# Attention with a sliding window and a mixing layer on one core: DMA transposes of q and k in three parts per batch, and batch 1's transposes in two bank pairs

## The chip, the cores and the metric

The kernel runs on one core of one Trainium2 chip. A time is the device time of one execution in microseconds; the kernel before took 301.77 us (median of 4 executions, 301.3 to 301.95). Engines are named as in the profile: PE is the matrix engine, PEld its weight load, DVE, ACT and POOL the vector, scalar and GpSimd engines, SP the engine that here only issues DMAs. Lines (L768) are those of the kernel before.

## The reference

Inputs are q, k and v of 8 batches, 8 heads, 576 positions and 64 head dimensions in float32, and two weights. Attention looks at most 127 positions back, with a bias that falls linearly with the distance; its output is the input of a two-layer block with g = h cos h between the layers.

```python
scores = scale * np.matmul(q, k.transpose(0, 1, 3, 2))
mask = (rel >= 0) & (rel < window)                    # window = 128
scores = np.where(mask, scores + bias[None], -1000000000.0)
attn = softmax(scores)
x = np.matmul(attn, v).transpose(0, 2, 1, 3).reshape(B * S, H * D)   # 4608 x 512
h = x @ w_in                                          # 512 -> 2048
out = (h * np.cos(h)) @ w_out                         # 2048 -> 512
```

## The kernel before

**Attention.** The 576 positions of a batch are four blocks of 128 and one of 64. The work is cut into units: a unit (b, pr, G) is batch b, a pair of heads pr, and two query blocks, 0 and 1 for G = 0, 2 and 3 for G = 1; a ninth unit (b, "t", None) is the tail, block 4 for all heads. A block of queries sees only its own block of keys and the one before. So G = 0 reads key blocks 0 and 1, G = 1 reads 1, 2 and 3, the tail reads 3 and 4. For each unit PE makes the scores (L538, the tail at L528), ACT takes the exponential (L568, L560), DVE multiplies by a mask with the bias in it (L592, L579), PE multiplies by v (L623 and L626, the tail L610 and L612), DVE divides by the sum (L664, L679, L652). The result xnat or xtail is brought to xT, channels on partitions, either by PE transposes (L692, L730) with an eviction (L702, L703, L739, L740), or by a DMA transpose from SP (`x_dma`, L753, the tail L748).

**The two layers.** They go over 9 chunks of 512 tokens. Chunk 0's first layer is `moe1_half` (L792) in halves of 256 tokens, the others `moe1` (L768); ACT makes the cosine (L774, L797), DVE the product gT (L778, L801). Chunk 0's second layer is plain (L853); the others use a scheme with seven products in place of eight (L909) and sums of gT and w_out made on DVE. SP stores the results (L865, L954).

**q and k.** The scores need them with the head dimension on partitions, in the tiles qt and kt (two of each, by the batch's parity). Batches 0 and 1 are loaded as rows and transposed on PE by `qk_transposes` (L481: blocks of 16 or 20 transposes into two PSUM banks, evicted at L498 or L499). From batch 2 on, POOL loads q and k with a conversion to bf16 (`load_nat`, L339, five DMAs each into qnat and knat), and SP issues two DMA transposes for each (`dma_transposes`): L350 for the four full blocks of all four head pairs, 16 blocks of 128 x 128, and L353 for the 64 positions of the tail. Both count on one semaphore, and the key `("tr", which, b % 2)` stands for both: `tkeys` makes every scores operation of the batch wait for the whole q and the whole k. `load_nat` of batch b + 2 writes over qnat and knat of batch b, so it waits for b's transposes; for batch 3 it waits for batch 2's transposes by an explicit key (L343).

**Order.** Each call of `op` records an operation with the keys that it reads and writes. Nothing is scheduled at run time: the table `STARTS` holds a start for each operation and, where an operation may run on ACT or DVE, which of the two. `Plan.schedule` sorts by it, and `Plan.emit` writes each engine's instructions in that order, with semaphore waits where the keys ask for them. Every engine works strictly in its order, SP and POOL (which issue the DMAs) too.

Of the kernel before, what the change touches and what calls it, by code (L numbers as in the profile page):

```python
# [16 lines left out]
NBLK = 5  # L17
# [13 lines left out]
    "c-pO24RBP|72cOXa(x5(I4W)~i!PU!n68h_l0Nn)ci$#JvTT>Qh5<sb{46Q06ag_HP0@nHLTijMGE9d;#FQ$-pI~Q%qT-BFY"  # L31
    "cW#GD1!*tv9_RN!730;7P7DBy<IjxyHU&ZC42Y0bI-l^obP<++_eaL+;Z(nNjm=Fn{E-hvv26ov#utlbwS5Rz**D4Fw`x*pT"
    "UBV^`+(7ocZasXYy75rdI*~@V_gyWw)jG2H!=pWYA@ZG2>cuRv5@Gp1~`N9uu;Y?k8>az8(mA2LG}y8DnmDmXKv07aJt#!dG"
    "b#T<xzIe5LQZkY(xYtI59Ro!-mSxEWTr8CvgIy<c2?HTnQ!iXs`~y*B9S7z<ffg|CyW=^i*+18UL~@&1aev~36X#RmzN9m|L"
    "h%0hq4uNR*Te9$uty#ng)CCAJ(4T>9B33!wc6NG+o_j|YGbpG$)WnW3t#QL$Tub(~45lmS~VkM;6q-!h#Xs|qVQ?F;LQ&eUp"
    "8dP`6COh6EW2X=jSr<AJSf!WD_3$c9A@paOklWGUCbu)g`n3Kfq;x`WXN7NEo9XHPj%$TXf$2T?3WgK8U-wWc7Ef8`=obc?T"
    "XdRv64G7j?$5+QSH3*~mT#-$tengJO$K#lWTGX>#O}1+GHZkZ>)346i3_dgP8=LJ&>7s7GRwBaQgT*zSE53MEB_DDr9FdU{j"
    "0GLyUkFNcXK9KdhEYTfeHf`XtJC40y$X@F>{5Wr`25iI#`jW$oV?0mv^OM)HOgq?(UWG-nmX$3IpGSee{AEwh;T)tLM6|t2E"
    "?<^rF9<=4>xF(cZWmu4#JYc(1aEe`APoOIExO=~M2<Q+^BAzSI1Rr?tim8eAXGfJHn5U{yu>`?oQfna`Ic1qF8NvYf3s(e1J"
    "DA4)zHOAc-M4Scrk@ldEN6xvebYB{>~Y^`Iq{>5y)cD(<lGW}FpS((2C2b>RuR@c2}eXYiJXwmKaXTl+vl7A+!oY|a=%_)*P"  # L40
    "1HKXG3(v8R+{ny#JW{7TY(&?nyMvD{TR8pHc=?!gxBV@-U7ku8d-gn%-%`Ma16?JZ*8Z&y2Qo{At=e8jL_*xu%105=FM=di@"
    "jnA99e}zUP+)|JRz6G;32H>^<Z&tiLW$^{JkqulP!<FHY1~6R>D^w!|49rxLW=oZAhLw>RNIUyQV5l|^S?>72F(5Tp&ca+RO"
    "TIM9f%Oc$|r_Oq5<DLw`+?>zZ#95XkRjvZL{s1_2gKXI(n4TJCXWtE|Mx_n;IHhIKu-KOmc^PQJU?OD)K9Q;Ot&+;HAAEsw{"
    "~b(%X+8w?`W&tC0X|K$U{kAOS0m19b#g<044~30(y59NS4iaiLd|gED*bkz0bHdWIUPUhZyV;AUs-f#PCRFuo5YHK4sv6LdH"
    "6iPdjP0quU7v>xX_T-dgW@hiCHiqh4%XQ1?Hrouv=hbPFsH7cI_(+8m%!ka%deDKXhpUNwK8$?;V6P;k=S8w%tF9wg(w}O+$"
    "z$Dq_^iHPsQ7Go;6^DyH|CI-o!ynzh!?oTJN00M>oNqItta{zsFyr;t+m1#*cYTQ98VNNA5Q+8OdlQnBROj(ZT9q=A@ne075"
    "M>%QM6sDr5DWGjNez{Vvdu`PXd8Q`&?z!e^5PN-wKg~1HS&NVV(LX{1#t(8>4cJlDlo?9)>F#(%W4ZW@hLIZxJ|oA)cR)Lv3"
    "<F^llvG{Gd_C(Kvb&$rr3E=HH8V<?->O<UkuU$#=l|_aB6=92KI@Q)N-(wu14tXeCo-=OUBt6>7rNeGe8;Ra*w5#<`%&uCKr"
    "eAypX`h9h&EAK~c-U&j$`Y5N-d6N)3D*e6{M_C!r&uRR?d3ZjME7nH7CExOhl&3M=F(SOd##QaFi?4ZrhFeM}Uw2T>+lcM=i"
    "#3)8@$FAy88Q$$!$Kumn`Q!wVC3yM4FG7yKAt{_wq-`bZb;3At!%8Z@ZDn<Q*8C-fG2+Ypcf-E)h$=;uom1q}LC~NV(QFaI#"  # L50
    "crKL`<eP+T#J3kY<K`ogQFi`VvFu>l2gsR|+H7;5*AOelH$&uvQ=5oPL#zr9@Ba(kZ#(i-5j^?*9ctAw*JB>=&7b2A4c$q*e"
    "9|4>FFa8F!Io(I-ukV-zGsZ}rXkI>?Z4Qvo$f7y=jUJe9C>Bm{%BO+u+hGvWTR6Hd=}jx88L$ihjqS;h}EZ{kw*BQgB0;>go"
    "+Z~h$Dp()Ho@T5#Ji8h;))5XtPm+VtErQ@yo{U#f`(Hd;)1)Jn67ZT$K2oHny~YP<4^}%R)lToeTI56?+ji_;qXIDAL5Apy*"
    "Q-9a6x#SRIN`_n}bfJ=lvxhv>BPJi<&vyY{I_B|}vBTw*Sj?OZn{1_eCV=wn7bXp7BqA)=k%WS$}6X<dd2=NX@8_{|JE0cRE"
# [166 lines left out]
def bass_alibi_sliding__then__act_gcu_kernel(  # L221
# [8 lines left out]
    with ExitStack() as ctx:  # L230
# [104 lines left out]
        def load_nat(which, src, b):  # L335
            fns = []
            for t in range(NBLK):
# [6 lines left out]
               dma=f"ldn{which}{b % 2}", occ=4400, lat=4500)  # L344

        def dma_transposes(b):
            for which in ("q", "k"):
                t = tr[which][b % 2][:, :].rearrange("p (c k t) -> p c k t", c=NBLK, k=NPAIR)
                fns = [
                    lambda e, t=t, which=which: e.dma_start_transpose(  # L350
# [769 lines left out]
```

The softmax here doesn't subtract the row's maximum and nothing guards it: scores larger than these inputs give would overflow.

## Time and profile before

| | |
|---|---|
| median of 4 executions | 301.77 us (301.3 to 301.95) |
| the profiled execution | 301.95 us, of which the span from first to last instruction is 300.2 |
| TensorE clock granted | 1.000 |
| busy: PE, DVE, ACT, POOL | 292.9, 240.5, 209.5, 95.0 us |
| software queue (POOL's DMAs) | 99344 packets, 18.10 MB |
| hardware queue (SP's DMAs) | 48976 packets, 19.54 MB |
| DMA transposes of q and k | 24: 12 of 16 blocks, 12 of the tail |
| qt, from issue to landing (min, median, max) | 2.4, 7.8, 13.2 us |
| kt, the same | 2.4, 7.4, 13.7 us |

How to read it: busy time and what ended the idle time stand by line and engine. The chain of work that ended last is followed back from the last instruction, at each step to what released it; "issue" in it is time in which the profile shows no engine that was waited for. A DMA is issued by SP or POOL, and the time in which the queue is busy with the issue (SPq) is not the time of the transfer: that ends with the landing. By stretches of the execution (columns: length, busy us and instructions of each engine, granted clock, mean busy DMA share, GB/s):

```profile
0.00:24.00 24.00, 20.39 (x270) 13.52 (x271) 16.02 (x52) 18.90 (x31) 22.42 (x36) 1.00 1.26 177
24.00:72.00 48.00, 48.00 (x468) 29.34 (x467) 38.00 (x71) 35.49 (x52) 18.82 (x23) 1.00 1.74 177
72.00:125.00 53.00, 52.89 (x599) 37.33 (x593) 46.66 (x99) 40.18 (x54) 29.59 (x37) 1.00 1.88 161
125.00:185.00 60.00, 59.38 (x664) 45.94 (x663) 53.17 (x107) 46.48 (x63) 24.16 (x29) 1.00 1.61 139
185.00:260.00 75.00, 74.87 (x659) 47.80 (x658) 60.36 (x110) 50.61 (x71) 0.00 (x0) 1.00 0.37 74
260.00:300.00 40.00, 37.35 (x279) 26.90 (x277) 26.24 (x44) 17.82 (x32) 0.00 (x0) 1.00 0.22 73
```

The first column of each bracketed pair is PE, then PEld, DVE, ACT and POOL.

### The profile page before, as it was taken

What the parts mean: (1) busy time and instruction counts of PE and PEld (TensorE: products, weight loads), DVE (VectorE), ACT (ScalarE), POOL (GpSimd) and SP (SyncE); (2) the same over time, 40 slices, a digit from 0 to 9 for tenths busy, and PEclk for the clock granted to TensorE, in tenths of its full rate; (3) what the DMA queues carried; (4) which work ended last, traced back from release to release, by engine and by line L of the source; (5) the groups of instructions that cost most, each with busy time, mean ns of one, the idle gap of its engine ahead of it and who ended that gap; (6) DMA issues with size and microseconds to landing.
All of it is one profiled execution on the core that took longest, in us unless ns stands there. A gap on an engine that the chain in (4) does not pass through costs nothing.

```text
span 300.2 us, 7125 instructions
## 1 busy us (share of the span) xinstructions
PE 292.9 (98%) x2925; PEld 200.8 (67%) x2925; DVE 240.5 (80%) x478; ACT 209.5 (70%) x300; POOL 95.0 (32%) x122
## 2 busy tenths in 40 slices
PE   8889999999999999999999999999999999999996
PEld 4568746547774688548888876568746865566685
DVE  3787678789977998899988879788978967685871
ACT  6887977398857788588768775778676945644432
POOL 7998230069956502760196004000000000000000
PEclk9999999999999999999999999999999999999999
DMA  7999999999999999999999999942304111120033
GB/s 142 181 200 210 206 165 174 145 160 186 172 133 138 174 156 178 159 173 167 139 110 144 147 115 158 159 78 64 98 27 99 44 30 52 37 76 31 0 124 122
DMA packets 148352, 38.09 MB, mean 127 GB/s; under 512 B 133984, under 2 KB 147040, under 8 KB 148320
## 3 DMA queue, kind: packets, MB, share of 16 engines
q0 software_dynamic: 99344, 18.10, 78.7%
q1 hardware_dynamic: 48976, 19.54, 36.0%
q8 instruction: 23, 0.38, 0.5%
q14 instruction: 9, 0.07, 0.1%
HBM read 36.70 MB, written 9.44 MB: 154 GB/s over the span
## 4 chain that ended last, share of the span: by engine, by line
PE 94%; DVE 2%; DMA 1%; issue 1%; ACT 0%; DVEq 0%; ACTq 0%
PE ps L768 37%; PE ps L909 33%; PE ps L538 5%; PE ps L792 5%; PE ps L853 5%; PE ps L623 3%; PE ps L626 2%; PE ps L481 2%; DMA ob<-in_q_dram 1%; PE ps L692 1%; PE ps L528 1%; PE ps L610 1%; PE ps L612 1%; DVE xnat L664 1%; DVE xT L740 0%
## 5 line engine op out<-in xcount | busy, mean ns | idle before, releaser
L768 PE MATMUL ps<-xT,w_inb 128*128 128x512 bf16 (+1 forms) x576 | 129.8, 356 | 0.0
L774 ACT ACTIVATE cos<-ps,halfpi 128x512 f32<-128x512 f32 x128 | 82.3, 686 | 46.3 <-PE ps L768 34.9
L778 DVE TENSOR_TENSOR gT<-ps,cos 128x512 f16<-128x512 f32 x128 | 83.0, 685 | 21.6 <-ACT cos L774 21.1
L768 PEld LDWEIGHTS ps<-xT,w_inb 128*128 128x128 bf16 x576 | 55.1, 98 | 39.8 <-DVE xnat L679 0.8
L568 ACT ACTIVATE p<-ps 128x768 bf16<-128x768 f32 (+1 forms) x64 | 55.6, 917 | 8.5 <-PE ps L538 7.5
L329 POOL DMA_DIRECT2D vp<-in_v_dram x40 | 34.0, 872 | 64.1 <-PE ps L626 51.2
L909 PE MATMUL ps<-wsum,gT 128*128 128x256 f16 x256 | 50.8, 273 | 0.1
L592 DVE TENSOR_TENSOR p<-p,emask 128x512 bf16<-128x512 bf16 (+2 forms) x88 | 39.0, 470 | 3.7 <-ACT p L568 3.3
L909 PE MATMUL ps<-w_outb,gT 128*128 128x256 f16 x256 | 39.7, 273 | 0.0
L909 PE MATMUL ps<-wsum,gsum 128*128 128x256 f16 x256 | 37.2, 273 | 0.0
L339 POOL DMA_DIRECT2D qnat<-in_q_dram x30 | 25.4, 902 | 17.4 <-DMA qt<-qnat 17.4
L909 PEld LDWEIGHTS ps<-wsum,gT 128*128 128x128 f16 x256 | 24.2, 97 | 9.1 <-DVE ob L933 0.8
L909 PEld LDWEIGHTS ps<-w_outb,gT 128*128 128x128 f16 x256 | 24.5, 98 | 8.4 <-ACT ob L929 0.3
L909 PEld LDWEIGHTS ps<-wsum,gsum 128*128 128x128 f16 x256 | 24.7, 98 | 4.6 <-ACT qrows L929 0.2
L339 POOL DMA_DIRECT2D knat<-in_k_dram x30 | 25.6, 928 | 6.2 <-DMA kt<-knat 3.8
L909 PE MATMUL ps<-w_outb,gsum 128*128 128x256 f16 x128 | 26.1, 273 | 0.0
L679 DVE TENSOR_TENSOR xnat<-ps,rec 128x512 bf16<-128x512 f32 x28 | 19.3, 690 | 1.3
L929 ACT ACTIVATE qrows<-ps 128x512 f32<-128x512 f32 (+1 forms) x18 | 9.9, 552 | 14.2 <-PE ps L909 14.1
L538 PE MATMUL ps<-qt,kt 64*128 64x128 bf16 (+1 forms) x320 | 18.4, 240 | 1.1 <-issue 0.6
L623 PE MATMUL ps<-vp,p 128*128 128x65 bf16 x256 | 18.0, 194 | 0.9 <-issue 0.5
L623 PEld LDWEIGHTS ps<-vp,p 128*128 128x128 bf16 x256 | 15.6, 97 | 4.3 <-issue 1.5
L626 PE MATMUL ps<-vp,p 128*128 128x65 bf16 x192 | 16.9, 193 | 0.0
(81 smaller groups left out, 334.2 us busy)
## 6 DMA issues: line engine op xcount, KB each, us to landing
out_dram<-ob SPq DMA_DIRECT2D x32, 256.0 KB, 4.3
vp<-in_v_dram POOLq DMA_DIRECT2D x32, 128.0 KB, 8.7
qnat<-in_q_dram POOLq DMA_DIRECT2D x24, 128.0 KB, 10.9
knat<-in_k_dram POOLq DMA_DIRECT2D x24, 128.0 KB, 14.4
w_inb<-in_moe_w_in_dram POOLq DMA_DIRECT2D x4, 512.0 KB, 10.8
w_outb<-in_moe_w_out_dram POOLq DMA_DIRECT2D x4, 512.0 KB, 22.2
out_dram<-ob SPq DMA_DIRECT2D x8, 128.0 KB, 1.8
qrows<-in_q_dram POOLq DMA_DIRECT2D x1, 576.0 KB, 15.6
```

The lines of the kernel that those rows point to most:

```text
L329: op("pool", [lambda e, t=t, rows=rows: e.dma_start(vp[b % 2][0:rows, t, :, 0:64], v[b, :, 128 * t:128 * t + rows, :].rearrange("h p d -> ...
L339: fns.append(lambda e, t=t, rows=rows: e.dma_start(nat[which][b % 2][0:rows, t, :, :], src[b, :, 128 * t:128 * t + rows, :].rearrange("h p ...
L538: ins = e.matmul(ps[:, banks[x], c0:c1], keys_ap(b, x, pr, kc), query_ap(b, x, pr, qb, 128 * nb), start=not added, stop=True, skip_group_c ...
L568: op("act", lambda e: e.activation(P[i][:, :, 0:hi], src_[:, :, 0:hi], ACTF.Exp, scale=0.125), w=held + [("P", i)], occ=920 if G else 691, ...
L592: op("dve", lambda e, p=p, m=m: e.tensor_tensor(p, p, m, ALU.mult), r=[("P", i), ("EM", h0), ("EM", h1)], w=[("P", i)] if n != 1 else [("P ...
L623: ins = e.matmul(o, P[i][:, x, d0:d0 + 128], V[:, kc, h, 0:65], start=True, stop=not two)
L626: ins = e.matmul(o, P[i][:, x, p0:p0 + 128], V[:, kc - 1, h, 0:65], start=False, stop=True)
L679: op("dve", lambda e: e.tensor_tensor(o, U[:, :, :, 0:64], rv[:, :, :, None].broadcast_to([128, 2, 4, 64]), ALU.mult), r=[("rec", n // 2 % ...
L768: op("pe", lambda e, kc=kc, c0=c0: e.matmul(ps[:, bank, c0:c0 + n], w_in[:, kc, 128 * fc:128 * fc + 128], xT[:, kc, (r0 + c0) % XR:(r0 + c ...
L774: op("act", lambda e: e.activation(cosb[ci][:, :], ps[:, bank, :], ACTF.Sin, bias=halfpi[:, 0:1]), r=["halfpi"], w=[("B", bank), ("cos", c ...
L778: op("dve", lambda e: e.tensor_tensor(gT[gi][:, fc, :], ps[:, bank, :], cosb[ci][:, :], ALU.mult), r=[("cos", ci)], w=[("B", bank), ("g", ...
L909: op("pe", lambda e, t=t, fc=fc, bk=bk: e.matmul(ps[:, bk, 256 * t:256 * t + 256], lhs(fc, t), rhs(fc), start=first and fc == 0 and (last ...
```

## The change

`dma_transposes` makes three DMAs for q and three for k per batch in place of two each: part 0 for blocks 0 and 1, part 1 for blocks 2 and 3 (8 blocks of 128 x 128 each), part 2 for the tail. Each part has a semaphore and a key of its own. `tkeys` makes a unit of G = 0 wait for part 0 of q and k, one of G = 1 for q's part 1 and k's parts 0 and 1, the tail for q's part 2 and k's parts 1 and 2. `load_nat` of batch 3 waits for part 1 of batch 2. In batch 1's transposes on PE, q now uses the banks `SB[0:2]` while k keeps `SB[2:4]`; before, both used `SB[2:4]`. The table `STARTS` is new, so the order on all engines is written anew.

```diff
-            op("pool", fns, r=[("tr", which, 0)] if b == 3 else [], w=[("nat", which, b % 2)],
+            op("pool", fns, r=[("tr", which, 0, "p", 1)] if b == 3 else [], w=[("nat", which, b % 2)],
                dma=f"ldn{which}{b % 2}", occ=4400, lat=4500)
 
         def dma_transposes(b):
-            for which in ("q", "k"):
-                t = tr[which][b % 2][:, :].rearrange("p (c k t) -> p c k t", c=NBLK, k=NPAIR)
-                fns = [
-                    lambda e, t=t, which=which: e.dma_start_transpose(
-                        t[:, 0:4, :, :].rearrange("p c k t -> p (c k) t"),
-                        nat[which][b % 2][:, 0:4, :, :].rearrange("p c h d -> p (c h d)")),
-                    lambda e, t=t, which=which: e.dma_start_transpose(
-                        t[:, 4, :, 0:64],
-                        nat[which][b % 2][0:64, 4, :, :].rearrange("p h d -> p (h d)")),
-                ]
-                op("sp", fns, r=[("nat", which, b % 2)] + ([("ktail", b % 2)] if which == "k" else []),
-                   w=[("tr", which, b % 2)], dma=f"tr{which}{b % 2}", occ=2500, lat=4300)
+            for part, (c0, c1) in enumerate(((0, 2), (2, 4), (4, 5))):
+                for which in ("k", "q"):
+                    t = tr[which][b % 2][:, :].rearrange("p (c k t) -> p c k t", c=NBLK, k=NPAIR)
+                    src_ = nat[which][b % 2]
+                    if part < 2:
+                        o = t[:, c0:c1, :, :].rearrange("p c k t -> p (c k) t")
+                        i = src_[:, c0:c1, :, :].rearrange("p c h d -> p (c h d)")
+                    else:
+                        o = t[:, 4, :, 0:64]
+                        i = src_[0:64, 4, :, :].rearrange("p h d -> p (h d)")
+                    op("sp", [lambda e, o=o, i=i: e.dma_start_transpose(o, i)],
+                       r=[("nat", which, b % 2)] + ([("ktail", b % 2)] if which == "k" else []),
+                       w=[("tr", which, b % 2, "p", part)], dma=f"tr{which}{b % 2}{part}",
+                       occ=3150 if part < 2 else 1300, lat=1900 if part < 2 else 500)
...
         def tkeys(u):
             b, _, G = u
             keys = [("tr", w_, b % 2) for w_ in ("q", "k")] + [("ktail", b % 2)]
+            parts = {"q": (0, 1, 2), "k": (0, 1, 2)}
+            if b >= BPE:
+                parts = {0: {"q": (0,), "k": (0,)}, 1: {"q": (1,), "k": (0, 1)},
+                         None: {"q": (2,), "k": (1, 2)}}[G]
+            keys += [("tr", w_, b % 2, "p", i) for w_ in ("q", "k") for i in parts[w_]]
...
                 for half in range(2):
-                    qk_transposes(1, "q", 0, half, SB[2:4])
+                    qk_transposes(1, "q", 0, half, SB[0:2])
                     qk_transposes(1, "k", 0, half, SB[2:4])
```

What the two tables of starts make of it, engine by engine:

- PE: the same 2925 matmuls in another order. In the head, the last pair group of batch 0's v products (16 matmuls at L623 and L626) stands behind eight L792 matmuls of feature chunks 4 and 6, which are the first to read the second quarter of w_in; before, it stood ahead of them. Batch 1's four blocks of transposes (L481) were q, k, q, k, each with other matmuls around it; they are now k, then q and k next to each other, then q.
- DVE has five evictions more and ACT five fewer: two of chunk 0's output, one of qt, two of xT.
- POOL has the same DMAs in the same order. The first `load_v` of batch 1 waits for a memset of vp's ones column that now stands later in DVE's order, behind the normalisation of batch 0's last pair units.
- SP has 36 DMA transposes of q and k in place of 24. Its order around batches 2 to 4 and 5 to 6 (q0 is part 0 of q; xT is one `x_dma`; xTt that of a tail):

```
batch 2 to 4, before: q2 k2 st st xTt(1) st st q3 k3 xTt(2) st q4 k4 st ...
              after:  q0 k0 q1 (batch 2) st xTt(1) st q2 st k1 st k2 (batch 2)
                      q1 k1 k0 q0 (batch 3) st q2 (batch 3) q2 (batch 4) k2 (batch 3) st
                      k0 q0 k2 (batch 4) st xTt(2) st k1 q1 (batch 4) ...
batch 5 to 6, before: xT xT st k6 xT xTt(4) xT xT q6 xT xT xT ...
              after:  xT xT st q1 k2 (batch 5) xTt(4) xT st xT xT xT
                      q0 k0 (batch 6) xT xT k1 (batch 6) ...
```

In the rows "before", q2 is both DMAs of q of batch 2, and so on; st is a store.

## The prediction

> **What bounds the kernel now.** I read the page first, then the chain of work that ended last, then the timeline of SP (the queue that issues every DMA transpose), then single tiles for the time from a DMA's issue to its landing.
>
> ```profile
> span 300.2 us, 7125 instructions
> ...
> PE 292.9 (98%) x2925; PEld 200.8 (67%) x2925; DVE 240.5 (80%) x478; ACT 209.5 (70%) x300; POOL 95.0 (32%) x122
> ...
> PEclk9999999999999999999999999999999999999999
> DMA  7999999999999999999999999942304111120033
> ```
>
> PE is the bound at full clock, and the change removes no matmul (the instruction counts of PE are equal). So only PE's waits can be won or lost. The DMA engines are busy until about 195 us; there a DMA's landing is far from its issue. The chain, where PE waits longest after its first 24 us:
>
> ```profile
> 176.89 0.98 PE ps L909 x9
> 177.87 0.62 issue
> 178.50 0.51 PE ps L538 x8
> ```
>
> L538 is the scores matmul; these are the first scores of batch 6. "issue" means that no engine released it. SP's timeline and the landings of qt say who did:
>
> ```profile
> 148.59 2.46 SPq L753 DMA_TRANSPOSE xT<-xnat  x2
> 151.09 0.58 SPq L954 DMA_DIRECT2D out_dram<-ob  x1
> 151.72 6.46 SPq L350 DMA_TRANSPOSE kt<-knat  x1
> 158.22 1.31 SPq L353 DMA_TRANSPOSE kt<-knat  x1
> 159.57 1.24 SPq L753 DMA_TRANSPOSE xT<-xnat  x1
> 160.85 1.26 SPq L748 DMA_TRANSPOSE xT<-xtail  x1
> 162.15 2.60 SPq L753 DMA_TRANSPOSE xT<-xnat  x2
> 164.79 6.11 SPq L350 DMA_TRANSPOSE qt<-qnat  x1
> 170.94 1.25 SPq L353 DMA_TRANSPOSE qt<-qnat  x1
> ```
>
> ```profile
> DMA to landing us min/median/max: 7.5/10.3/13.2
> ```
>
> The last line is tile qt between 160 and 182 us: two DMAs, the 16-block one 13.2 us, the tail 7.5 us. 170.94 + 7.46 = 178.40, and PE's weight load starts at 178.47. So one DMA transpose holds PE. The last L909 starts at 177.60 and takes 0.11 at this rate, so PE stood from 177.71 to 178.50, 0.79 us, of which 0.10 is what any switch to scores costs (in the timeline five L853 from 38.40 at 0.216 end at 39.48, and L538 starts at 39.58 with no wait).
>
> **The change part by part.** The sum is against the profiled execution, 301.95 us (span 300.2, 1.75 around it). That is 0.18 above the median of 301.77, whose executions spread from 301.3 to 301.95.
>
> *Three parts per batch.* Half a transpose (8 blocks) is in no row of before. Bounds: 1.25 us (the tail, 4 narrow blocks) and 6.1 us (16 blocks in this stage, if a half cost as much as the whole). Between them I take 3.1, half of 6.1: the tail at 1.25 and the 16 blocks at 6.11 grow with the blocks, about 0.4 us a block. After the end of its issue a DMA took about 7 us to land here (170.9 to 178.0); in the quiet stage near 193.5 it took 2.6 (issue 1.85, landing 4.4 after its start). I take 7.
>
> Batch 6 in the new order of SP, from the same 148.6: two xT 2.46, a store 0.58, q part 1 of batch 5 3.1, k part 2 of batch 5 1.3, the tail's xT 1.26, one xT 1.25, a store 0.58, three xT 3.8, q part 0 of batch 6 3.1, k part 0 3.1. Sum 20.5, so the issue ends at 169.1 and part 0 lands at 176.1. The scores want it at about 177.9. It is there 1.8 us early, and the wait of 0.69 goes. Late next is nothing near: the x_dma behind it would land at about 178.6 and is read by L768 from 182.3. With 6.1 for each of the three halves it lands 9 us later and the wait is 7 us. With 1.25 it is 5 us earlier and no more is won: -0.69 is the most.
>
> *Twelve more DMAs on SP.* In the row of four xT transposes at 243.16 (5.07 us) SP issues one per 1.27 us while each needs about 2.3 to land, so they overlap. At most 12 x 1.25 = 15 us of issue, spread over 120 us of a queue that has waits; hidden by the early issue of what is behind them. Without that cover an xT would come late and hold L768. [...]
>
> *The head.* Until 24 us PE waits for loads. The second quarter of w_in decides here:
>
> ```profile
> L361 POOL DMA_DIRECT2D w_inb<-in_moe_w_in_dram x1: 813/813/813, 10.4 to 10.4; - x1
> ...
> DMA to landing us min/median/max: 9.9/9.9/9.9
> ```
>
> ```profile
> 19.84 0.20 PE L623 MATMUL ps<-vp,p 128*128 128x65 bf16 x1 [0.39 <-DVE xT L740]
> ...
> 20.36 1.16 PE L792 MATMUL ps<-xT,w_inb 128*128 128x256 bf16 x9
> ...
> 22.78 0.77 PEld L792 LDWEIGHTS ps<-xT,w_inb 128*128 128x128 bf16 x8 [0.28 <-ACT xT L739]
> ```
>
> It lands at 20.31, and L792 on it starts at 20.36. Before, the last 16 L623/L626 matmuls of batch 0's pair units are just done by then. In the new order they stand behind eight L792 that need this quarter, so PE does them after 20.36 instead of in the wait: 16 x 0.030 = 0.48, with the switch +0.50. Between -0 (if eight other matmuls filled the wait as well; the order shows none) and +0.6. Against this, L792 of the second half waited at 22.5 for xT, 0.17 of PE's time; in the new order more than 15 matmuls stand between that transpose and its reader: -0.17.
>
> *Batch 1's transposes in two bank pairs.* Rows: L481 x20 takes 0.68, x16 takes 0.57, so 0.028 each and 0.12 fixed, and 0.10 to enter. Four separate blocks become three (q's first and k's second are neighbours): -0.22. It is nothing if k's banks are not yet read (an eviction takes 0.9), which k's earlier block makes unlikely.
>
> ```profile
> 29.02 0.68 PE ps L481 x20
> ...
> 34.62 0.57 PE ps L481 x16
> ```
>
> *Five evictions go from ACT to DVE* (two ob, one qt, two xT): about 3.0 us on DVE, which has 60 us idle; no row shows DVE as PE's limit after 24 us. Zero; 3.0 if that cover were gone.
>
> *POOL's loads.* load_v of batch 1 now waits for a memset that stands later on DVE, some 5 us; these loads landed 25 us after issue because of the queue ahead of them, so zero. load_nat of k for batch 3 waits for k's part 1, which SP issues behind three stores: POOL's chain moves by 5 to 7 us. Who waits for that is batch 4, below.
>
> Sum: 301.95 - 0.69 + 0.50 - 0.17 - 0.22 = 301.37. **Forecast 301.4 us**, 0.12% under the median.
>
> **The rivals.**
>
> *Slower: batch 4 comes late.* Before, k of batch 4 was loaded and transposed so:
>
> ```profile
> L339 POOL DMA_DIRECT2D knat<-in_k_dram x5: 878/1049/1057, 79.5 to 83.0; - x5
> ...
> DMA to landing us min/median/max: 13.7/16.1/16.8
> ```
>
> The last landed at 83.0 + 16.8 = 99.8; its transposes landed at 115.7 (108.0 + 7.7), 1.5 us before the scores at 117.2. After, POOL issues this load 5 to 7 us later. If the backlog eats the delay it lands at 99.8 again; if it passes in full, at 106.8. Behind it stand k part 0 and q part 0 (6.2) and 7 us to land: 113.0 to 120.0. The scores want it at 117.6. In the middle there is no wait; at the end 2.4 us, and the xT of batch 2's tail, now behind k part 2 (2.6 more), would be 3.7 us late for L768. It decides when the load lands later than about 104. Price 2.5 to 3.7, so about 304.4. For it: the new wait of POOL. Against it: 20 of batch 4's 40 blocks no longer stand before these scores, and a queue with 17 us of backlog forgives a late issue.
>
> *No effect:* part 0 of batch 6 lands no earlier, since SP has 12 more issues, and the wait stays: 301.95 + 0.11 = 302.1. For it: all DMA shares the same busy engines. Against: 28 blocks instead of 40 stand before these scores.
>
> *More gain:* PE's other waits after 24 us go too, as all orders were written anew; the chain has one more of this kind, and about 0.3 near 109 us:
>
> ```profile
> 246.39 0.40 issue
> 246.79 0.70 DVE ob L933
> ```
>
> Together some 0.5: 300.9. Nothing in the diff aims at them.
>
> **How the numbers follow.** Forecast 0.58, late batch 4 0.17, no effect 0.10, more gain 0.15. A measurement of this kernel tells about 0.2% (0.6 us) from no change, so the limits are 301.17 and 302.37. The forecast case has a spread of some 0.4 and falls under 301.17 in about 0.28 of it: faster 0.16 + 0.15 = 0.31. Slower: late batch 4 and 0.01 of the forecast's, 0.18. The rest, 0.51, is the same. The range reaches from just below "more gain" to inside the late case, 300.8 to 303.0, with about 0.05 under and 0.11 over it; the forecast alone would have 300.9 to 301.9.
>
> **What would show it.** Right: no "issue" of 0.6 before the first scores of batch 6; the half transposes at 3 us of issue in the busy stage; the 16 L623/L626 after 20.4 us; three L481 blocks near 34 to 38 us; PE's busy time the same. Wrong: halves that cost as much as wholes, "issue" before L538 near 117.6 or before L768 near 119, or a new wait of L768 for a late xT.

## The result, and the profile after

The changed kernel takes 302.42 us (median of 51 executions, 301.05 to 304.69), the kernel before, beside it, 301.79 (72 executions, 300.98 to 303.04). The ratio is 1.0023 with a 95% interval of 1.0014 to 1.0031: slower by a quarter of a per cent, where 301.4 had been forecast.

The median hides two groups. Of 52 executions whose clock is listed, the profiled one among them, 36 had TensorE's full clock and a median of 302.11; 16 had a mean granted clock of 0.993 or 0.994 and a median of 303.18. The profiled execution, 301.84 us (span 300.1, 1.74 around it), is of the first group and 0.58 below the median. It shows less than the whole loss, and what it does not show had to come from other runs.

Lines are from here on those of the changed kernel: the first layer is L799 and L775 (before: L792 and L768), the second L860 and L916 (L853, L909), the scores L545 (L538), p times v L630 and L633 (L623, L626), batch 0's and 1's transposes L483 (L481), the transposes of xnat on PE L737 (L730) and by DMA L760 (L753), the exponentials L575 and L567 (L568, L560), the mask L599 (L592), the normalisations L671 and L686 (L664, L679), the evictions to xT L746 and L747 (L739, L740), and chunk 0's cosine L804 (L797). qrows and krows hold q and k of batches 0 and 1 as rows.

The page and the stretches of the changed kernel (columns as before: length, PE, PEld, DVE, ACT and POOL busy, granted clock, DMA share, GB/s):

```profile
span 300.1 us, 7163 instructions
...
PE 291.8 (97%) x2925; PEld 199.4 (66%) x2925; DVE 242.4 (81%) x483; ACT 207.2 (69%) x295; POOL 95.0 (32%) x122
```

```profile
0.00:24.00 24.00, 18.45 (x259) 11.96 (x260) 14.62 (x49) 17.34 (x28) 15.35 (x27) 1.00 1.26 173
24.00:72.00 48.00, 48.00 (x469) 29.61 (x467) 39.47 (x76) 35.56 (x51) 20.96 (x25) 1.00 1.64 170
72.00:125.00 53.00, 53.00 (x601) 36.89 (x600) 47.68 (x100) 38.52 (x52) 33.52 (x40) 1.00 1.83 157
125.00:185.00 60.00, 60.00 (x662) 46.15 (x660) 53.70 (x105) 47.03 (x64) 25.14 (x30) 1.00 1.71 142
185.00:260.00 75.00, 75.00 (x671) 48.18 (x670) 61.51 (x114) 51.62 (x73) 0.00 (x0) 1.00 0.47 87
```

From 24 to 260 us PE has no idle time left: 53.00, 60.00 and 75.00 us busy where it had 52.89, 59.38 and 74.87, so 0.86 us were won there; the rest behind 260 us did not change (37.33 us busy, before 37.35). In the first 24 us it was busy for 18.45 us in place of 20.39, and did 259 matmuls in place of 270. In this profile, what was won there was lost in the head, the stretch up to 24 us.

The chain around batch 6's first scores, and SP's timeline ahead of them (in an SP line: start, time in the queue, line, instruction):

```profile
177.65 1.20 PE ps L916 x11
178.85 0.44 PE ps L545 x8
```

```profile
164.53 1.33 SPq L357 DMA_TRANSPOSE qt<-qnat  x1
165.90 3.48 SPq L357 DMA_TRANSPOSE kt<-knat  x1
169.42 2.78 SPq L760 DMA_TRANSPOSE xT<-xnat  x2
```

The "issue" of 0.62 us before these scores is gone. Part 0 of q landed at 171.8 and part 0 of k at 175.4 (7.3 and 9.5 us after their start by the trace's landings), the scores came at 178.8. Behind the parts stand two DMA transposes of xnat, which will matter.

The head, in PE's timeline (start, duration, line; in brackets the idle time before and who ended it):

```profile
10.19 0.75 PE L483 MATMUL ps<-ident,krows 128*64 128x128 bf16 x20 [1.12 <-DMA krows<-in_k_dram]
...
15.58 0.28 PE L799 MATMUL ps<-xT,w_inb 128*128 128x256 bf16 x1 [1.23 <-ACT p L575]
...
20.65 0.40 PE L737 MATMUL ps<-ident,xnat 128*128 128x128 bf16 x4 [0.92 <-DVE xnat L671]
```

Before, PE waited for neither:

```profile
9.30 0.34 PE L538 MATMUL ps<-qt,kt 64*128 64x256 bf16 x4
9.59 0.51 PE L450 MATMUL ps<-dif,ob 128*128 128x256 bf16 x4
10.03 0.34 PE L538 MATMUL ps<-qt,kt 64*128 64x256 bf16 x4
10.30 0.75 PE L481 MATMUL ps<-ident,krows 128*64 128x128 bf16 x20
...
14.52 0.77 PE L538 MATMUL ps<-qt,kt 64*128 64x256 bf16 x12
15.22 0.28 PE L792 MATMUL ps<-xT,w_inb 128*128 128x256 bf16 x1
```

Scores filled the time until krows had landed (10.16), and twelve more that until w_in's first quarter had (14.67). In the new order the last twelve stand behind the first L799. The name behind the second wait above is a coincidence: an exponential ended at 15.58, but by the trace w_in's first quarter landed at 15.53. In a second profile of the same kernel, taken later (303.24 us, full clock), the wait has its right name:

```profile
15.83 0.28 PE L799 MATMUL ps<-xT,w_inb 128*128 128x256 bf16 x1 [1.49 <-DMA w_inb<-in_moe_w_in_dram]
```

The hole goes on through ACT. The scores that its next exponentials need come behind the first L799, so ACT starts them at 16.34, and the chain that ended last runs over ACT until PE's next p times v:

```profile
15.98 0.34 PE ps L545 x6
...
16.34 1.94 ACT p L575 x2
18.28 0.92 ACT ptail L567
...
21.78 0.28 ACT xT L746
```

The third wait, 0.92 us at 20.65, stands with the same length in all 13 profiles with the new head and in none of the six with the old one. No run removed it, so its price is not known.

Why the quarter lands later stands in POOL's and DVE's timelines of the changed kernel:

```profile
6.23 1.76 POOL L329 DMA_DIRECT2D vp<-in_v_dram  x2 [0.81 <-DVE vp L397]
7.97 0.77 POOL L363 DMA_DIRECT2D w_inb<-in_moe_w_in_dram  x1
```

```profile
4.83 0.43 DVE L321 CAST qrows<-ob 128x512 bf16<-128x512 f32 x1 [0.49 <-DMA ob<-in_q_dram]
...
5.65 0.27 DVE L397 MEMSET vp<- 64x256 uint32 x1
```

and of the kernel before:

```profile
5.51 1.76 POOL L329 DMA_DIRECT2D vp<-in_v_dram  x2
7.25 0.77 POOL L361 DMA_DIRECT2D w_inb<-in_moe_w_in_dram  x1
```

```profile
4.63 0.27 DVE L395 MEMSET vp<- 64x256 uint32 x1
4.94 0.43 DVE L321 CAST qrows<-ob 128x512 bf16<-128x512 f32 x1
```

Batch 0's first load of v waits for the memset of vp's zero rows. The memset stood ahead of qrows' cast and now stands behind it, and the cast waits for q's own load. POOL stands for 0.81 us, and the loads behind it, w_in's first quarter too, are issued 0.72 us later. The landing scatters from run to run: issued at 7.16 to 7.31 us it came between 14.39 and 15.14 in eleven profiles, issued at 7.90 to 7.97 between 14.44 and 15.79 in six.

The second profile shows one more wait. DVE's timeline and the chain there:

```profile
180.06 0.69 DVE L686 TENSOR_TENSOR xnat<-ps,rec 128x512 bf16<-128x512 f32 x1 [1.35 <-DMA xT<-xnat]
```

```profile
168.06 3.06 SPq L357
...
171.16 1.39 SPq L760
...
172.59 7.44 DMA xT<-xnat
...
181.08 0.61 DVE p L599
...
181.74 0.20 PE ps L630
```

L686 writes the normalised output of a pair of units into an xnat buffer. There are eight, so it must wait until the DMA transpose that reads the old content has landed, and that transpose now stands in SP's queue behind q's and k's part 0 of batch 6. It landed at 180.03 here; in the first profile at 177.47, 0.9 us before L686 wanted it. The mask behind L686 is late with it, and PE waits 0.89 us before its p times v.

### The profile page after: what moved, and what is told of

Read it like the earlier page. It is cut to its first block, busy times and chain, and to the rows that moved or that the text cites. A ratio compares the mean times of both kernels' runs of the same rounds, so it can differ in the third digit from the quotient of the medians.

```text
span 300.1 us, 7163 instructions
## 1 busy us (share of the span) xinstructions
PE 291.8 (97%) x2925; PEld 199.4 (66%) x2925; DVE 242.4 (81%) x483; ACT 207.2 (69%) x295; POOL 95.0 (32%) x122
## 4 chain that ended last, share of the span: by engine, by line
PE 93%; ACT 3%; DMA 2%; POOL 1%; issue 0%; POOLq 0%; ACTq 0%
PE ps L775 37%; PE ps L916 33%; PE ps L545 5%; PE ps L860 5%; PE ps L799 4%; PE ps L630 3%; PE ps L633 2%; DMA krows<-in_k_dram 2%; ACT p L575 1%; PE ps L699 1%; PE ps L483 1%; PE ps L617 1%; PE ps L619 1%; PE ps L535 1%; ACT L804 0%
## 5 line engine op out<-in xcount | busy, mean ns | idle before, releaser
L775 PE MATMUL ps<-xT,w_inb 128*128 128x512 bf16 (+1 forms) x576 | 129.7, 356 | 0.0
L775 PEld LDWEIGHTS ps<-xT,w_inb 128*128 128x128 bf16 x576 | 55.3, 98 | 41.2 <-DVE gT L785 1.0
L575 ACT ACTIVATE p<-ps 128x768 bf16<-128x768 f32 (+1 forms) x64 | 55.6, 917 | 11.7 <-PE ps L545 7.7
L916 PE MATMUL ps<-wsum,gT 128*128 128x256 f16 x256 | 48.6, 273 | 0.0
L916 PE MATMUL ps<-w_outb,gT 128*128 128x256 f16 x256 | 41.1, 273 | 0.0
L599 DVE TENSOR_TENSOR p<-p,emask 128x512 bf16<-128x512 bf16 (+2 forms) x88 | 39.3, 471 | 1.8 <-ACT p L575 1.0
L916 PE MATMUL ps<-wsum,gsum 128*128 128x256 f16 x256 | 39.1, 273 | 0.0
L916 PEld LDWEIGHTS ps<-w_outb,gT 128*128 128x128 f16 x256 | 24.5, 98 | 8.3 <-issue 0.3
L916 PEld LDWEIGHTS ps<-wsum,gT 128*128 128x128 f16 x256 | 24.4, 97 | 8.4 <-issue 0.6
L916 PEld LDWEIGHTS ps<-wsum,gsum 128*128 128x128 f16 x256 | 24.4, 98 | 4.8 <-DVE gsum L850 0.3
L916 PE MATMUL ps<-w_outb,gsum 128*128 128x256 f16 x128 | 26.4, 273 | 0.0
L686 DVE TENSOR_TENSOR xnat<-ps,rec 128x512 bf16<-128x512 f32 x28 | 19.3, 690 | 1.1
L545 PE MATMUL ps<-qt,kt 64*128 64x128 bf16 (+1 forms) x320 | 18.5, 240 | 0.5 <-DVE kt L501 0.4
L630 PE MATMUL ps<-vp,p 128*128 128x65 bf16 x256 | 18.0, 194 | 0.2 <-ACT xT L746 0.2
L630 PEld LDWEIGHTS ps<-vp,p 128*128 128x128 bf16 x256 | 15.6, 98 | 2.7 <-issue 0.6
L633 PE MATMUL ps<-vp,p 128*128 128x65 bf16 x192 | 16.9, 193 | 0.0
```

Of the source, the lines that this page charges most:

```text
L545: ins = e.matmul(ps[:, banks[x], c0:c1], keys_ap(b, x, pr, kc), query_ap(b, x, pr, qb, 128 * nb), start=not added, stop=True, skip_group_c ...
L575: op("act", lambda e: e.activation(P[i][:, :, 0:hi], src_[:, :, 0:hi], ACTF.Exp, scale=0.125), w=held + [("P", i)], occ=920 if G else 691, ...
L599: op("dve", lambda e, p=p, m=m: e.tensor_tensor(p, p, m, ALU.mult), r=[("P", i), ("EM", h0), ("EM", h1)], w=[("P", i)] if n != 1 else [("P ...
L630: ins = e.matmul(o, P[i][:, x, d0:d0 + 128], V[:, kc, h, 0:65], start=True, stop=not two)
L633: ins = e.matmul(o, P[i][:, x, p0:p0 + 128], V[:, kc - 1, h, 0:65], start=False, stop=True)
L686: op("dve", lambda e: e.tensor_tensor(o, U[:, :, :, 0:64], rv[:, :, :, None].broadcast_to([128, 2, 4, 64]), ALU.mult), r=[("rec", n // 2 % ...
```

## The experiments

Three suspects: the head (krows' transposes without cover, that is, with no other work of PE ahead of them; w_in late by the memset), the xnat buffer, and the clock. The first rival was that the parts themselves cost. "Full" counts executions at a clock of 0.999 or 1.000, "low" those at 0.989 to 0.994; the ratio is to the kernel before on the same chip.

| kernel | full: count, median (range) | low: count | ratio (95%) |
|---|---|---|---|
| changed | 36, 302.11 (301.05 to 303.62) | 16 | 1.0023 (1.0014 to 1.0031) |
| changed, taken again | 8, 302.05 (301.73 to 303.24) | 4 | 1.0027 (1.0004 to 1.0050) |
| three parts alone, old order | 12, 301.41 (300.88 to 301.56) | 0 | 0.9977 (0.9964 to 0.9990) |
| old order to 28 us | 12, 302.98 (302.37 to 303.82) | 0 | 1.0028 (1.0013 to 1.0043) |
| before, new order to 28 us | 2, 303.84 and 304.61 | 4 | 1.0089 (1.0065 to 1.0113) |
| changed, one unit ahead | 5, 301.65 (301.22 to 303.43) | 7 | 1.0049 (1.0018 to 1.0080) |
| changed, ten xnat buffers | 6, 302.15 (301.62 to 302.53) | 6 | 1.0025 (1.0010 to 1.0041) |
| changed, one xnat transpose ahead | 9, 301.82 (300.96 to 302.40) | 3 | 1.0004 (0.9982 to 1.0025) |
| old order to 24 us | 9, 301.02 (300.89 to 301.40) | 0 | 0.9972 (0.9962 to 0.9982) |
| the same, ten buffers | 9, 300.82 (300.53 to 302.52) | 0 | 0.9973 (0.9957 to 0.9989) |
| changed, memset ahead | 12, 301.66 (301.07 to 302.68) | 0 | 0.9985 (0.9961 to 1.0008) |
| old order to 24 us, memset behind | 12, 302.04 (300.54 to 303.82) | 0 | 1.0001 (0.9982 to 1.0021) |
| changed, memset and unit ahead | 11, 301.48 (301.02 to 302.19) | 1 | 0.9997 (0.9979 to 1.0015) |
| changed, hole before w_in filled | 12, 302.12 (301.84 to 303.54) | 0 | 1.0011 (0.9997 to 1.0024) |
| memset ahead, ten buffers | 8, 301.93 (301.71 to 302.17) | 4 | 1.0007 (0.9991 to 1.0022) |
| memset and xnat transpose ahead | 7, 301.70 (301.26 to 301.90) | 5 | 0.9994 (0.9966 to 1.0021) |
| memset, unit and xnat transpose ahead | 12, 301.37 (300.85 to 302.55) | 0 | 0.9987 (0.9969 to 1.0006) |
| the one above it, wait for krows filled | 10, 301.60 (301.21 to 303.05) | 2 | 1.0008 (0.9985 to 1.0031) |

The last row fills the wait in the kernel with memset and xnat transpose ahead. The kernel before itself had 3 low executions in 146. Orders are changed by changing the table of starts alone. Measured together on one chip each were the four rows from 'three parts alone' on; the four from 'ten xnat buffers' on; the four from 'memset ahead' on; the next two, some six minutes later on the same chip; and the last two with 'changed, taken again'.

**The three parts alone.** Their code, in the old order and with the old banks:

```diff
 SP, old order:
-q (blocks 0 to 3), q tail; k (blocks 0 to 3), k tail
+q part 0, q part 1, q part 2; k part 0, k part 1, k part 2
-qk_transposes(1, "q", 0, half, SB[0:2])
+qk_transposes(1, "q", 0, half, SB[2:4])
```

> The three parts alone: the changed kernel with the old order of everything and the old banks for batch 1; the three DMAs of q stand where the old two of q stood, those of k likewise. If the parts do what the prediction says, the wait before batch 6 (0.79 us, 0.69 over a plain switch) goes and nothing else moves: 301.79 - 0.7 = 301.1 (300.9 to 301.3). Rival 'parts cost': twelve more DMAs in SP's queue delay an xT or a load, 302.0 to 302.4.

Measured: 301.41, ratio 0.9977, none low, and the narrow spread of 0.68 us (the kernel before, beside it: 301.29 to 303.24). That is what the prediction's first term says; the interval, 0.10 to 0.36%, holds its 0.69 us. In the profile the first scores of batch 6 follow an L916 with no wait, and q's part 0 had landed at 173.6. The rival that the parts cost has fallen: its 302.0 to 302.4 lies above every execution.

**Old order to 28 us, and new order to 28 us on the kernel before.**

```diff
 starts of all operations that the old table places before 28 us:
-new table
+old table (and the engine it chose)
```

> The changed kernel, but every operation that the old table starts before 28 us stands in the old order (and on the old engine). Theory 'head': what the change lost is the order of the first 28 us, where PE waits 1.12 us for the second piece of krows (landing 10.14) with no scores placed ahead of it, and ACT's exponentials come late after it; then the wait before batch 6 stays gone and this kernel takes 301.79 - 0.79 = 301.0 (300.8 to 301.3), and no execution shows a granted clock of 0.994. Rival 'parts': the twelve more DMA transposes and the later loads hold PE in executions that the profile did not catch; then the head costs little and this kernel stays at 302.4, a third of its executions at a clock of 0.994 as in the changed kernel.

```diff
 kernel before; operations that the new table places before 28 us:
-old table
+new table (and the engine it chose)
```

> The kernel before, but every operation that the new table starts before 28 us stands in the new order (and on the new engine); q and k in whole transposes, batch 1's banks as before. Theory 'head': 301.79 + 1.0 = 302.8 where the clock is full, and a third of the executions at a clock of 0.994 with 1.1 us more, so a median of 302.8 to 303.2. Rival 'parts': 301.8, no execution at 0.994.

Measured: 302.98 with none low, and 305.03 with four of six low. Neither number can be used for its size. The cut split a group of chunk 0's features: in the first, PE waits 1.34 us before an L799 at 30.05 that this kernel alone has, and it has a wait for L686 like the one above (1.14 us on DVE, 0.68 on PE at 182.01). The signs count: the new head on the kernel before makes it slower and brings the low clock, the old head takes the low clock away. The second also shows where the clock falls (columns as above):

```profile
15.00:16.00 1.00, 0.00 (x0) 0.00 (x0) 0.87 (x4) 0.68 (x1) 1.00 (x3) 1.00 2.48 155
16.00:17.00 1.00, 0.68 (x10) 0.45 (x11) 0.65 (x2) 0.00 (x0) 1.00 (x2) 1.00 2.04 173
17.00:18.00 1.00, 1.00 (x10) 0.36 (x8) 0.05 (x1) 0.91 (x1) 1.00 (x2) 0.52 1.39 206
18.00:19.00 1.00, 1.00 (x21) 0.71 (x19) 0.32 (x2) 0.96 (x2) 0.14 (x1) 0.50 1.22 203
19.00:20.00 1.00, 1.00 (x13) 0.67 (x8) 1.00 (x2) 0.94 (x2) 0.00 (x0) 0.50 1.26 208
20.00:21.00 1.00, 1.00 (x12) 0.83 (x11) 0.31 (x2) 0.98 (x2) 0.00 (x0) 0.78 1.23 206
```

PE stood from 14.5 to 16.3, as w_in's first quarter landed at 16.28 there. From 17.0 to 20.4 the granted clock was one half. The profile with ten buffers, also a low one, has the same picture 1 us earlier: a hole that ends at 15.7 and half the clock from 16.0 to 19.4.

**One unit ahead.**

```diff
 PE:
  transposes of qrows, second piece (L483 x20)
+ biases and scores of heads 6 and 7, G = 0 (L452 x4, L545 x4)
  transposes of krows, second piece (L483 x20)
  biases and scores of heads 4 and 5, G = 0
- biases and scores of heads 6 and 7, G = 0
 ACT: exponential of heads 6 and 7 ahead of that of heads 4 and 5
```

> The changed kernel, but PE does the biases and scores of one unit (batch 0, heads 6 and 7, G = 0) ahead of the transposes of krows' second piece, and ACT its exponential ahead of that of heads 4 and 5. Theory 'head': PE's wait for krows falls from 1.12 to about 0.4 us and the third exponential starts at 10.6 instead of 11.7; some 0.6 of the head's 1.0 us comes back, 301.8 in the median, and fewer or no executions at 0.994. Rival 'parts': no change, 302.4. A second rival, 'ACT': the wait is not what counts, since ACT is the chain from 16.3 to 21.8 us anyway (two exponentials, the tail's, a table load, two cosines); then the gain is under 0.2.

Measured: 303.74, seven of twelve low (four of them at 0.989, where the low ones elsewhere have 0.993 or 0.994; its profile is of an execution at full clock), 301.65 in the five at full clock. The wait for krows nearly went as meant (the scores ahead end at 10.45, the transposes start at 10.59), but the first L799 came at 15.76, 0.05 us after w_in's landing (15.71) and behind 1.31 us of idle PE: the time won piled up in the next hole. So krows alone was not the limit of the head.

**The xnat buffer.**

```diff
-NX = 8
+NX = 10
```

> The changed kernel with ten xnat buffers in place of eight. Theory 'xnat': the DMA transpose of batch 4's heads 4 and 5 (G = 1) now stands in SP's queue behind q's and k's part 0 of batch 6, and the normalisation near 178 us that writes the same xnat buffer waits for its landing, in some executions more than in others; the unit that follows gets its mask late and PE waits before its p times v. With ten buffers that writer comes two units later: executions at full clock fall from a median of 302.11 to 301.1 to 301.6, those at a clock of 0.994 stay a third and about 1.1 to 1.7 above them. Rival 'head only': the spread of the changed kernel is made in the first 24 us, this wait is an accident of two other profiles; then 302.4 in the median as before.

```diff
 SP:
+xT <- xnat, batch 4, heads 4 and 5, G = 1
 q part 0, k part 0 of batch 6
 xT <- xnat, batch 5, heads 6 and 7, G = 0
-xT <- xnat, batch 4, heads 4 and 5, G = 1
```

> The changed kernel with one instruction moved: in SP's queue the DMA transpose of batch 4's heads 4 and 5 (G = 1) stands ahead of q's and k's part 0 of batch 6 in place of behind them. Theory 'xnat': it lands at about 170 in place of 177.5 to 180.3, k's part 0 lands 1.3 us later, about 176.7, still 2 us before the scores at 178.8; the same as with ten buffers, full-clock executions at 301.1 to 301.6. Rival 'head only': 302.4. Rival 'queue': the delay of part 0 brings back PE's wait before batch 6's scores, 302.4 or more.

Measured: 302.63 and 302.01; at full clock 302.15 and 301.82 against 302.11. Neither profile has a wait of L686, and with the transpose moved ahead k's part 0 still landed at 175.96, before the scores, so the rival 'queue' has fallen. The median did not fall to 301.6, so the theory that this wait makes the spread was wrong in its size. It may make the upper end: of the full-clock executions with the new head, 14 of 84 were above 302.5 in the kernels without a repair of it, up to 303.62, and 3 of 52 in the six with one. These kernels differ in their heads too, so the counts alone do not show it.

**Old order to 24 us, with eight and with ten buffers.**

```diff
 starts of all operations that the old table places before 24 us:
-new table
+old table (and the engine it chose)
```

> The changed kernel, but every operation that the old table starts before 24 us stands in the old order (a cut at 28 us split a group of chunk 0's features in two and made a wait of its own). Theory 'head' and 'xnat' together: no execution at a clock of 0.994; 1.0 us comes back in the head, but PE then reaches 178 us earlier and waits longer there for the late landing, 0.5 to 1.2 us: 301.5 to 302.2. Theory 'head only': 301.0 to 301.2.

> Both: the old order up to 24 us and ten xnat buffers. If the head and the xnat wait are all that the change lost, it takes 301.0 (300.8 to 301.3), no execution at 0.994, with a spread as narrow as that of the three parts alone (300.88 to 301.56). If something else in the new order costs, 301.7 or more.

Measured: 301.02 and 300.82, none low, ratios 0.9972 and 0.9973. This is the decisive pair: with the old order of the first 24 us the change gains 0.28%, so its whole loss comes from the new order of these 24 us. The expected wait for xnat did not come with eight buffers: DVE reached L686 at 177.26, but SP was earlier too (part 0 of q issued at 162.37 in place of 164.53), and the transpose had landed at 175.3. The two kernels can't be told apart. Both beat the kernel before and the changed one.

**The memset, in both directions.**

```diff
 DVE, changed kernel:
  memset p (L415), memset vp ones (L396)
+ memset vp zero rows (L397)
  two of the scaled identities (L433), cast of qrows (L321), three of L433
- memset vp zero rows (L397)
```

> The changed kernel with one DVE instruction moved: the memset of vp's zero rows (L397, 0.27 us) stands behind the first memsets, ahead of qrows' cast, as it did before. Theory 'memset': POOL's first load of v waits for it, POOL stands 0.7 to 1.1 us, every load behind it is issued that much later, and w_in's first quarter lands at 15.5 to 16.3 in place of 14.6 to 15.1; PE's first L799 starts 0.05 us after that landing, behind a hole of 1.4 to 2.0 us. Now w_in's quarter is issued at 7.25 and lands at about 14.7, the first L799 starts near 15.0, 0.6 us come back in the full-clock executions (301.4 to 301.6 in place of 302.11), and the shorter hole leaves few or none at a clock of 0.994. Rival 'ACT': ACT's exponentials, table load and cosines are the chain up to 21.8 us whatever PE does; then under 0.2 us, 302.2 in the median.

```diff
 DVE, old order to 24 us:
- memset vp zero rows (L397)
  cast of qrows (L321), three of L433
+ memset vp zero rows (L397)
```

> The reverse, on the kernel with the old order up to 24 us (301.02): only the memset of vp's zero rows is moved, behind qrows' cast and three multiplications, where the change has it. Theory 'memset': w_in's first quarter lands 0.7 to 1.0 us later, at 15.3 to 16, the hole ahead of the first L799 grows, 0.5 to 0.9 us are lost, 301.5 to 301.9 at full clock, and some executions show 0.994 with 1.1 us more. Rival 'order of PE': the new head is slow by its order on PE; then no change, 301.0.

Measured: one memset of 0.27 us, moved ahead, takes the changed kernel from 302.42 to 301.66 with none of 12 low, at full clock from 302.11 to 301.66; moved behind, it takes the other from 301.02 to 302.04, none low. In the first, POOL issues w_in's quarter at 7.16, it lands at 14.59, and the first L799 waits for an eviction of xT instead:

```profile
7.16 0.77 POOL L363 DMA_DIRECT2D w_inb<-in_moe_w_in_dram  x1
```

```profile
15.00 0.27 PE L799 MATMUL ps<-xT,w_inb 128*128 128x256 bf16 x1 [0.45 <-ACT xT L746]
```

In the second it lands at 15.56, and PE waits for two quarters of w_in, the first and the last (landed at 26.34):

```profile
15.61 0.28 PE L799 MATMUL ps<-xT,w_inb 128*128 128x256 bf16 x1 [0.40 <-DMA w_inb<-in_moe_w_in_dram]
...
26.39 8.15 PE L799 MATMUL ps<-xT,w_inb 128*128 128x256 bf16 x72 [0.60 <-DMA w_inb<-in_moe_w_in_dram]
```

The rival 'ACT' (a gain under 0.2) and the rival 'order of PE' (no loss) have both fallen. The reverse lost 1.0, more than the 0.5 to 0.9 expected: the estimate had the first quarter alone, and the two waits are 1.0 us together. Its executions spread from 300.54 to 303.82, and its profile has the wait for xnat as well (0.19 us of PE at 180.5).

**Memset and unit together.**

```diff
 the edits of 'memset ahead' and 'one unit ahead'
```

> The changed kernel with both: the memset of vp ahead, and one unit's biases, scores and exponential ahead of the transposes of krows' second piece. If the head's loss is w_in's late landing and PE's wait for krows, this takes what the old order up to 24 us takes, 301.0 to 301.3, with no execution at 0.994. If only the memset counts, it equals the kernel with the memset alone.

Measured: 301.59, one low: no better than the memset alone, and its profile has a wait for xnat (PE 0.43 us at 180.4).

**The hole filled.**

```diff
+keep()   # four matmuls 128 x 512 on emask into OB[0], not read
 for i in range(NFC):
     moe1_half(c, i // 8, i % 8, (OB + SB)[i] if i < 6 else (OB + SB)[i % 4])
```

> The changed kernel with four more matmuls (128 x 512 on emask, into the bank that the first L799 overwrites, nobody reads them) between the transposes at 14.1 and the first L799 at 15.58 us: 0.85 us of the hole are filled, the landing of w_in stays. Theory 'clock': the granted clock falls to a half for one stretch of 3.4 us (as in the profile of the new head on the kernel before, 17.0 to 20.4) in executions in which PE stood too long in the hole; with the hole filled no or nearly no execution shows 0.994, the full-clock ones stay as they were, 302.1 in the median (301.05 to 302.8). Rival 'chance': the clock does not follow from the hole; a third stays at 0.994 and the median at 302.4.

Measured: 302.12, none of 12 low; the full-clock median did not move. If the share were 16 in 52 here too, none in 12 would have a chance of (36/52)^12, about 1 in 80. But the share is not steady: the four kernels measured together here had 1 low in 48, filled or not, and the head of 'memset ahead', with 0 in 12 here, had 9 in 24 some six minutes later on the same chip (next). The unaltered changed kernel was not among the four. So it is not shown that the filler took the low clock away. In the profile w_in's first quarter had landed at 14.44 already, and it was the filler that held the first L799:

```profile
14.77 1.04 PE L426 MATMUL ps<-emask 128*128 128x512 bf16 x4 [0.36 <-ACT xT L746]
15.64 0.27 PE L799 MATMUL ps<-xT,w_inb 128*128 128x256 bf16 x1
```

**What is left after the memset.**

```diff
 'memset ahead'
-NX = 8
+NX = 10
```

> The memset ahead and ten xnat buffers. With the memset alone the executions at full clock lie in two heaps, 301.07 to 301.34 and 301.55 to 302.68; the old order up to 24 us gave 300.89 to 301.40. Theory 'xnat': the upper heap is the wait of the normalisation near 178 us for the DMA transpose behind part 0 of batch 6; with ten buffers it goes, median 301.2, none above 301.6. Rival 'head': the upper heap is made in the first 24 us, by the landings that PE waits for without cover; then both heaps stay, median 301.6.

```diff
 the edits of 'memset ahead' and 'one xnat transpose ahead'
```

> The memset ahead and the one DMA transpose of xnat moved ahead of part 0 of batch 6 in SP's queue, eight buffers. Theory 'xnat': the same as with ten buffers, median 301.2, none above 301.6. Rival 'head': both heaps stay, median 301.6.

Measured: 302.09 with four low and 301.83 with five low. At full clock both have a narrow spread (301.71 to 302.17, 301.26 to 301.90), but around 301.9 and 301.7, not 301.2; the lower heap is gone as well, and neither theory has that. Their profiles show one cause of the difference: krows landed at 10.87 and 10.44 (10.34 in the profile with the memset alone), and PE's first L799 came at 15.53 and 15.10 (15.00). So in this order, without cover, the scatter of krows' landing passes on in full, 0.53 and 0.10 us; whether it makes the medians is not shown. The low clock had come back too, so the memset does not remove it for good.

**All three repairs; the wait for krows filled; the changed kernel again.**

```diff
 the edits of 'memset ahead', 'one unit ahead' and 'one xnat transpose ahead'
```

> The changed kernel with all three repairs of order: the memset of vp ahead, one unit's biases, scores and exponential ahead of the transposes of krows' second piece, and the DMA transpose of xnat ahead of part 0 of batch 6. If these three are what the change lost, it comes near the kernel with the old order up to 24 us (301.02): 301.1 to 301.4, no execution above 301.9 at full clock, at most one at 0.994. If something else in the head counts too, it stays with the two repairs of the memset and the xnat transpose, 301.7 to 301.9.

```diff
 'memset and xnat transpose ahead'
+if n: keep()   # four matmuls 128 x 512 on emask into UB[0], not read
 qk_transposes(0, "k", n, 0, UB)
```

> The kernel with the memset ahead and the xnat transpose ahead (301.83, five of twelve executions at 0.994), and four matmuls (128 x 512 on emask, into a bank that the transposes of krows overwrite, nobody reads them) in PE's wait for krows, which was 1.46 us there. Theory 'clock': with the hole before 14 us already short, it is the wait for krows that lets the clock fall; filled, no or one execution shows 0.994 and the full-clock ones stay at 301.7. Rival: the clock does not follow from this hole, four to six executions at 0.994.

```diff
 (no edit)
```

> The changed kernel unaltered, beside the two others on the same chip in the same hour: 302.1 at full clock, a third at 0.994 and 303.2, by all theories. It tells whether the share at 0.994 differs from hour to hour.

Measured: 301.37 with none low, 301.71 with two low, and 302.40 with four low. The three repairs give back 1.05 of the 1.40 us between 302.42 and 301.02; none of these 12 executions was low, and one, at 302.55, was above the 301.9 expected. The last 0.35 us are not explained; PE's wait of 0.92 us for L671 is still there. With the wait for krows filled, two of twelve low lie between the theory (none or one) and its rival (four to six), and decide nothing.

## Why the prediction was wrong

Forecast were 301.4 us and a gain; measured were 302.42 and a loss. The part that the change aims at did what was foreseen. What failed is the step on the head, together with that on POOL's loads; a third, on what comes late next, cost less.

**Right: batch 6.** The half transposes took 1.33 and 3.48 us of SP's queue where 3.1 was taken (all halves and tails: 1.17 to 5.09); part 0 landed at 175.4, foreseen 176.1; the wait went. That the time is so near is partly luck: SP came to part 0 of q 1.6 us later than in the sum, and the two halves together took 1.4 us less. The three parts alone gave 0.23% (0.10 to 0.36), which holds the 0.69 us.

**Right: twelve more DMAs cost nothing in line.** The step took this from the overlap of the four xT transposes at 243.16 in the profile of before: one issue per 1.27 us, landings 2.3 to 3.1 us after their starts. The run with the parts alone shows it: with the twelve DMAs more and the old order it took 301.41 us, 0.9977 of the kernel before.

**Right: batch 4 is not late.** Its load of k landed at 102.1 by the trace, before the point of 104 from which the rival would decide; part 0 of q landed at 113.1, the scores came at 118.5.

**Wrong: "The head".** This term was mis-sized. The prediction had +0.50 - 0.17; measured, the new order up to 24 us costs 302.11 - 301.02 = 1.09 us at full clock (1.2 if each is set against the kernel before beside it, 301.79 and 301.92), and in 16 of 52 executions the low clock adds another 1.07. The step considered one landing, that of the second quarter of w_in, and not the two before it. In the changed kernel that landing (20.30) held nobody: its first reader came at 20.89, behind the wait for L671. The other two were in the profile of before: krows' second piece landed at 10.16, covered by the scores of two units ahead of it; the first quarter of w_in landed at 14.67, half a microsecond before its first use and covered by twelve scores. The new order puts one of the two units behind the transposes of krows and the twelve scores behind the first L799, and the quarter landed 0.86 us later in the profile, past its use.

**Wrong: "POOL's loads".** It followed a memset that moved on DVE to the load of batch 1 that waits for it, and rightly priced that at zero: the load was issued 7.4 us later (24.39) and landed 0.85 us later (43.58). The other memset of the same tile, for batch 0, moved as well, by 1.0 us, and was not followed. It holds POOL for 0.81 us, and w_in's first quarter, issued 0.72 us later, landed 0.86 us later in the profile: here the delay passed on. This single instruction is the largest part of the loss that was shown: -0.76 us in the median when put back (ratio 0.9985 in place of 1.0023; -0.45 us at full clock, and the rest goes with the low clock, which those 12 executions did not show), +1.02 when put behind (1.0001 in place of 0.9972).

**Wrong: "Late next is nothing near".** The sum had the DMA transpose behind part 0 land at 178.6 and looked at the one who reads xT, L768 from 182.3. It also frees an xnat buffer, and L686 writes that buffer at 178.4. The landing was foreseen within 1.1 and 1.4 us (177.5 in one profile, 180.0 in another); the one who waits was missed. The step "no row shows DVE as PE's limit after 24 us" fell with it. It costs PE 0.2 to 1.2 us in some executions (seen in profiles of five kernels), nothing in others.

**The clock** was not in the prediction at all, as no row of before had less than 1.00.

**One sign of being right did not come:** PE's busy time was to stay the same and fell from 292.9 to 291.8 us with the same 2925 matmuls. The traces do not say why, and nothing above rests on it.

**Open.** The bank pairs of batch 1 (-0.22) were not run alone. The profile has the three blocks that were foreseen, q and k next to each other at 36.84 and 37.42, but whether they gain can't be said: the old order up to 24 us and the parts alone differ by less than their intervals. Why the clock falls is not shown. It came with the new head (52 of 190 executions low, against 0 of 54 in the five changed kernels with the old head and 3 of 146 in the kernel before) and was seen in two profiles, both times behind the hole before w_in. The low clock was rarer with the memset ahead (12 of 72, against 40 of 118 with it behind the cast in the new head), but the same head gave 0 in 12 and 9 in 24 on one chip, so such counts depend on when they were taken.

## What to carry to other kernels

Where all orders are written anew, compare the head engine by engine, and for each load that PE waits for list what is ahead of its issue, down to a memset on another engine, and what PE has to do until it lands. Of a DMA that moves back in a queue, ask not only who reads its result but who may overwrite its source. One profiled execution below the median shows a part of the loss; look at the clock and span of all executions, and profile again, before explaining the median.

## What the runs showed of the hardware

A stretch of idle TensorE time of 1.6 to 1.8 us in the head was followed by 3.4 us at half the granted clock (17.0 to 20.4 in the kernel before with the new order to 28 us, 16.0 to 19.4 in the changed one with ten buffers); four of six executions of the first program and six of twelve of the second were low, the others not. In the 3 us that end near the fall PE was busy for 0.46 + 0.00 + 0.68 = 1.14 us in one and 1.00 + 0.04 + 0.31 = 1.35 us in the other; the profile of the changed kernel, with 0.89 + 0.35 + 0.42 = 1.66 us from 13 to 16 us, kept its clock. But so did that of the memset ahead with ten buffers, with 0.73 + 0.40 + 0.08 = 1.21 us from 8 to 11 us, so the busy share of such a stretch alone does not decide.

The first loads' landings move from run to run with the same issue times: krows' second piece, issued at 4.70 or 4.71, landed between 9.84 and 10.90 in the profiles of these kernels. In the order with the memset ahead, where PE has no other work until that landing, it was passed on: with a landing 0.53 us later (10.87 in place of 10.34), PE's first L799 came 0.53 us later (15.53 in place of 15.00).
